# Local and downsampled attention with two MLP layers: loads and GpSimd adds join the written order of the opening

## The chip, the cores and the metric

The kernel runs on one core of one Trainium2 chip. The metric is the device time of one execution in microseconds. Five engines matter here: PE (TensorE) multiplies, ACT (ScalarE) and DVE (VectorE) do the elementwise work, POOL (GpSimd) adds, and SP (SyncE) issues nearly all the DMAs.

## The reference

Four batches, eight heads, 576 positions, head size 64. The output of attention is a local part plus a coarse part; it runs through two MLP layers over all 2304 tokens.

```python
q_d, k_d, v_d = means of q, k, v over groups of 4 positions        # 144 of them
out_d     = softmax(scale * q_d @ k_d.T) @ v_d
out_up    = repeat(out_d, 4)                                       # back to 576
out_local = softmax(where(|i - j| < 4, scale * q @ k.T, -1e6)) @ v
x = (out_up + out_local) as 2304 x 512
h = x @ w_in            # 512 -> 2048
x = (h * sigmoid(1.702 * h)) @ w_out
h = x @ w2_in
y = where(h > 0, h, exp(min(h, 0)) - 1) @ w2_out
```

The weights arrive as 64-bit floats, and the kernel turns them into pairs of single-precision parts on the chip.

## The kernel before, in words

**Units.** Attention goes by unit: one batch and two heads (a head pair, four per batch). Of batch 0 a unit is split: `e0` to `e3` are windows 0 to 3 of its four head pairs (64 rows by 70 keys each) and its downsampled half, `l0` to `l3` are windows 4 to 8. `r0` to `r3` are the four head pairs of batch 1. The other batches come later, between the blocks of the first MLP layer, and are laid out by a planner that the change does not touch.

**A unit's steps** are tokens with the unit's name behind them. `Tq`/`Tk` turn a piece of q or k on PE (`turn_piece`, L506), `Cq`/`Ck` copy it from PSUM on ACT (L518; for `Cq.e0` on DVE, L516), `Sq`/`Sk` sum four positions on DVE (L522). `QK` makes the local scores (L550 mask, L559 product), `NM` their negative maximum on DVE (L586), `EW` the exponentials on ACT (L623). `QD`, `ND`, `NS`, `EC` are the same for the downsampled scores (L602, L609, L614, L630). `W`, `MS`, `MP` weigh both by the reciprocal of their sums on DVE (L661, L662, L665). `PD`/`PC` and `PT`/`PTC` turn the weights (L686/L694 and L704/L709/L711), `PVD` and `DN` make the downsampled result (L720, L728), `PV` and `X` the local one and the sum (L741, L756). `PVD` needs `vd`, the sums of four positions of v: for each of the unit's two heads (a half) one load of a tile `vr` (L469) and three additions on GpSimd (L474, L476). `PV` needs `vw`, the windows of v, four DMAs per unit (L486).

**The weights** come in chunks of 512 KB (`wst1i`, `wst1o`; L188, L193). `A1` (ACT, L212), `D1` and `DS` (DVE, L215), `D2` (DVE, L230), `A3` (ACT, L237) and `D3` (DVE, L241) convert one.

**The first MLP layer** runs in blocks of 256 or 512 tokens. In the opening blocks 0 and 1 go together: `H.s.p` is half p of step s of the first product (L993), `TH`, `ST`, `GH`, `GL` its gate (L1002, L1006, L1012, L1019), `Y.s.h` half h of the second product (L1060). Steps 0 to 7 cover 256 tokens and two chunks of weights, steps 8 to 15 both blocks and one chunk. `XH`/`XL` split the attention result into a high and a low part (L384, L388). `*N` is N filler products of 448 columns on PE (`keep_busy`, L1104), whose result nobody reads.

**What sets the order.** `OPENING` (L66 to L107) lists the tokens of blocks 0 and 1; a loop issues them one after the other inside `manual_schedule`, which keeps the written order on PE, ACT and DVE. For SP and GpSimd the order is the framework's. Loads have no tokens: those of the early units, six weight chunks and the first `vw` of a late unit stand in a fixed block ahead of the table (L1115 to L1133), and each further one hangs on a step: a weight chunk on `D2`, the next unit's q and k on the fourth turning, its `vw` on `PV`, a later unit's `vr` and its additions on `DN` (L730). The pool `att` has one tile `vr` for the units `r*`, and one tile `vw` that `e0`, the late units and the `r*` take in turn.

Of the kernel before, what the change touches and what calls it, by code (L numbers as in the profile page):

```python
# [50 lines left out]
LOADS = 6  # L51
# [20 lines left out]
    W.e0 ND1.e3 EW.e3 *1 PD0.e1 MP.e0 NS.e3 W.e2 PD0.e0 EC.e3 MS.e0 PD1.e0 PTC.e1 MP.e2 *1 PT.e0 PC0.e1 MS.e2
    PC0.e0 PD0.e2 PC1.e0 W.e3 PD1.e1 PD1.e2 PC0.e2 DS.1 PT.e2 PC1.e2 PTC.e0 PVD.e0 A1.1 MP.e3 PVD.e2 PC1.e1 DN.e0
    MS.e3 A1.2 PD0.e3 PTC.e2 PD1.e3 A3.0 PT.e3 D1.2 DN.e2 PVD.e1 PC1.e3 D2.1 PV.e2 DN.e1 PTC.e3 PC0.e3 PV.e0 X.e2
    DS.2 PV.e1 D1.3 PV.e3 X.e1 PVD.e3 D2.2 XH.01 XH.02 QK.l1 D3.0 A3.1 X.e0 A3.2 QK.l0 XL.02 A1.3 XL.01 NM.l1
    XH.00 D1.4 DN.e3 NM.l0 DS.3 EW.l0 D3.1 XL.00 D1.5 EW.l1 *11 H.0.0 W.l0 D2.3 H.0.1 MS.l0 A1.4 X.e3 PTc.l0
# [10 lines left out]
    A1.15 ST.5 QD0.r1 A3.14 D1.15 H.7.0 D3.13 DS.15 Ma.r1 D3.14 QD1.r1 A1.16 ST.4 H.7.1 A1.17 D2.15 GH.4 D1.16
    A3.15 H.6.0 ND1.r1 DS.16 ND0.r1 NS.r1 D3.15 EC.r1 H.6.1 D1.17 D2.16 MS.r0 A1.18 QKb.r1 A3.16 D1.18 PD1.r0
    Y.2.0 DS.17 Mb.r1 D3.16 PC1.r0 GL.4 PTa.r0 A1.19 D1.19 Tq0.r2 TH.6 Y.2.1 D2.17 DS.18 PTCa.r0 ST.6 A3.17 PVD.r0
    DS.19 D2.18 H.8.0 D3.17 Cq0.r2 D2.19 A3.18 Tq1.r2 H.8.1 A3.19 D3.18 DN.r0 A1.20 D3.19 PTb.r0 GH.5 D1.20 Y.3.0  # L90
    Cq1.r2 Na.r1 PTCb.r0 GL.5 EWa.r1 Nb.r1 Tk0.r2 Sq.r2 Y.3.1 EWb.r1 D1.21 TH.7 D1.22 Tk1.r2 Y.4.0 EWc.r1 ST.7
    D1.23 A1.21 H.9.0 W.r1 Ck1.r2 D1.24 Ck0.r2 MP.r1 GH.6 Y.4.1 Sk.r2 A1.22 GL.6 DS.20 PD0.r1 MS.r1 QD0.r2 PC0.r1
    Y.5.0 GH.7 ND0.r2 D2.20 DS.21 QD1.r2 A3.20 H.9.1 ND1.r2 NS.r2 D2.21 EC.r2 D1.25 Y.5.1 D3.20 TH.8 GL.7 A1.23
    PTc.r0 PVa.r0 PTCc.r0 DS.22 ST.8 QKa.r2 Xa.r0 D1.26 GH.8 Y.6.0 A3.21 Ma.r2 D2.22 TH.9 PD1.r1 DS.23 D3.21
    QKb.r2 GL.8 H.10.0 PC1.r1 Mb.r2 A1.24 ST.9 A3.22 Tk0.r3 Nb.r2 Tq0.r3 Na.r2 Ck0.r3 Y.6.1 D1.27 Cq0.r3 D2.23
    EWa.r2 PVD.r1 D1.28 A3.23 Tq1.r3 D3.22 Y.7.0 DN.r1 Cq1.r3 D1.29 DS.24 D3.23 PVb.r0 D1.30 Tk1.r3 Xb.r0 H.11.0
# [22 lines left out]
def kernel(  # L119
# [275 lines left out]
    class Unit:  # L395


        def __init__(self, b, hp, w0, w1, down=None):
# [36 lines left out]
        def load_qk(self):  # L435
            self.raw = []
            b, hp = self.b, self.hp
            if self in turned:
# [11 lines left out]
            for nm, src in (("q", q), ("k", k)):  # L450
                r = self.t([96, 6, 2, D], f"raw{nm}")

                queue = nc.scalar if self in early[:2] and nm == "k" else nc.sync
                for j in range(2):
                    queue.dma_start(
                        out=r[:, :, j, :], in_=src[b, 2 * hp + j].rearrange("(p t) d -> p t d", t=6)
                    )
                self.raw.append(r)
        def add_vd(self):

            b, hp = self.b, self.hp
            self.vd = self.t([HALF, 2, 2, D], "vd", bufs=2)
            for j in range(2):
                tag = ("gh", "gl", "gh", "g")[self.hp] if j == 0 else ("gh", "gl", "gl", "g")[self.hp]
                if self in early:
                    r = gpool.tile([HALF, 2, 4, D], F32, tag=tag, name=f"vr{j}_{self.n}", bufs=2 if tag == "g" else None)
                else:
                    r = att.tile([HALF, 2, 4, D], F32, tag="vr", name=f"vr{j}_{self.n}")
                nc.sync.dma_start(  # L469
                    out=r.rearrange("g c r d -> g c (r d)"),  # L470
                    in_=v[b, 2 * hp + j].rearrange("(c g r) d -> g c (r d)", g=HALF, r=4),
                )
                vd = self.vd[:, :, j, :]
                nc.gpsimd.tensor_tensor(out=vd, in0=r[:, :, 0, :], in1=r[:, :, 1, :], op=ALU.add)  # L474
                for i in (2, 3):
                    nc.gpsimd.tensor_tensor(out=vd, in0=vd, in1=r[:, :, i, :], op=ALU.add)  # L476
# [919 lines left out]
```

## Time and profile before

| what | value |
|---|---|
| median of 3 runs | 975.35 us (974.5 to 976.1) |
| the profiled execution, its own time | 974.49 us |
| its span | 972.3 us, mean granted TensorE clock 0.981 |
| PE busy in the span | 948.0 us, 97% |
| DVE, ACT, POOL busy | 503.8, 466.6, 60.8 us |
| first product of the MLP (`H.0.0`) | at 49.95 us |
| last product of a unit of the opening (`PVb.r3`) | at 190.01 us |

The profiled execution is 0.86 us under the median. Granted clock 1.00 means 2.4 GHz and 0.50 means 1.2 GHz. In the views of the trace an idle time in brackets stands before the work that followed it, with what that work was waiting for.

### The profile page before, as it was taken

What the parts mean: (1) busy time and instruction counts of PE and PEld (TensorE: products, weight loads), DVE (VectorE), ACT (ScalarE), POOL (GpSimd) and SP (SyncE); (2) the same over time, 40 slices, a digit from 0 to 9 for tenths busy, and PEclk for the clock granted to TensorE, in tenths of its full rate; (3) what the DMA queues carried; (4) which work ended last, traced back from release to release, by engine and by line L of the source; (5) the groups of instructions that cost most, each with busy time, mean ns of one, the idle gap of its engine ahead of it and who ended that gap; (6) DMA issues with size and microseconds to landing.
All of it is one profiled execution on the core that took longest, in us unless ns stands there. A gap on an engine that the chain in (4) does not pass through costs nothing. (4 is left out here: it accounts for less than half of the span.)

```text
span 972.3 us, 14685 instructions
## 1 busy us (share of the span) xinstructions
PE 948.0 (97%) x5773; PEld 775.6 (80%) x5773; DVE 503.8 (52%) x900; ACT 466.6 (48%) x1115; POOL 60.8 (6%) x117
## 2 busy tenths in 40 slices
PE   8978999999999999999999999999999999999998
PEld 5758987777777778888888978877888888888897
DVE  5888997676654543223225898884223222322232
ACT  5667999464343532232225566664334333433343
POOL 4330110201111010000000000000000000000000
PEclk9588999999999999999999999999999999999999
DMA  9587712153222204010007921002001100100010
GB/s 192 162 232 205 232 31 55 46 116 64 52 55 46 70 20 144 1 43 1 1 1 240 366 88 43 1 12 77 1 1 38 39 1 1 55 0 1 1 44 22
DMA packets 113332, 67.97 MB, mean 70 GB/s; under 512 B 80752, under 2 KB 102768, under 8 KB 113264
## 3 DMA queue, kind: packets, MB, share of 16 engines
q1 hardware_dynamic: 110896, 66.46, 24.3%
q10 hardware_dynamic: 2368, 0.59, 0.4%
q8 instruction: 45, 0.74, 0.3%
q14 instruction: 23, 0.19, 0.1%
HBM read 57.59 MB, written 9.44 MB: 69 GB/s over the span
## 5 line engine op out<-in xcount | busy, mean ns | idle before, releaser
L1245 PE MATMUL o<-whl2o,g2h 128*128 128x512 f32 x576 | 181.0, 394 | 2.4 <-ACT ye L1072 2.1
L1196 PE MATMUL h<-x2h,whl2i 128*128 128x512 f32 (+1 forms) x640 | 159.3, 371 | 0.0
L1060 PE MATMUL y<-g1h,whl1o 128*128 128x512 f32 (+1 forms) x512 | 156.2, 371 | 0.0
L993 PE MATMUL h<-xh,whl1i 128*128 128x512 f32 (+1 forms) x640 | 147.1, 354 | 2.4 <-DVE g L1006 2.4
L1206 DVE SCALAR_TENSOR_TENSOR g<-e,h 128x512 f32<-128x512 f32 (+1 forms) x80 | 50.7, 634 | 177.9 <-ACT e L1204 177.6
L1196 PEld LDWEIGHTS h<-x2h,whl2i 128*128 128x128 f32 x640 | 114.7, 189 | 22.7
L1245 PEld LDWEIGHTS o<-whl2o,g2h 128*128 128x128 f32 x576 | 107.2, 189 | 27.1 <-ACT ye L1072 2.5
L993 PEld LDWEIGHTS h<-xh,whl1i 128*128 128x128 f32 x640 | 105.8, 190 | 19.4 <-DVE g L1006 3.3
L1203 ACT ACTIVATE e<-h 128x512 f32<-128x512 f32 (+1 forms) x80 | 44.3, 554 | 158.3 <-PE h L1196 158.3
L1245 PE MATMUL o<-whl2o,g2l 128*128 128x512 f32 x288 | 113.1, 393 | 0.0
L1060 PEld LDWEIGHTS y<-g1h,whl1o 128*128 128x128 f32 x512 | 92.4, 189 | 16.3 <-issue 1.2
L1006 DVE SCALAR_TENSOR_TENSOR g<-g,h 128x512 f32<-128x512 f32 x64 | 43.8, 684 | 118.9 <-ACT g L1002 118.9
L1002 ACT ACTIVATE g<-h 128x512 f32<-128x512 f32 x64 | 38.1, 596 | 122.7 <-PE h L993 115.9
L1060 PE MATMUL y<-g1l,whl1o 128*128 128x512 f32 (+1 forms) x256 | 93.7, 366 | 0.0
L1196 PE MATMUL h<-x2l,whl2i 128*128 128x512 f32 (+1 forms) x320 | 79.6, 370 | 0.0
L993 PE MATMUL h<-xl,whl1i 128*128 128x512 f32 (+1 forms) x320 | 77.6, 354 | 0.0
L1213 DVE TENSOR_TENSOR g2l<-g,g2h 128x512 fp32r<-128x512 f32 (+1 forms) x80 | 51.7, 646 | 36.8 <-ACT g2h L1211 21.6
L1211 ACT ACTIVATE g2h<-g 128x512 fp32r<-128x512 f32 (+1 forms) x80 | 47.1, 589 | 42.8 <-DVE g L1206 42.7
L1196 PEld LDWEIGHTS h<-x2l,whl2i 128*128 128x128 f32 x320 | 56.7, 188 | 11.0
L1245 PEld LDWEIGHTS o<-whl2o,g2l 128*128 128x128 f32 x288 | 54.4, 189 | 12.0
L993 PEld LDWEIGHTS h<-xl,whl1i 128*128 128x128 f32 x320 | 53.2, 191 | 7.3 <-issue 0.4
L1019 DVE TENSOR_TENSOR g1l<-g,g1h 128x512 fp32r<-128x512 f32 x64 | 44.2, 691 | 27.7 <-ACT g1h L1012 27.4
(128 smaller groups left out, 1326.2 us busy)
## 6 DMA issues: line engine op xcount, KB each, us to landing
wst1i<-in_moe_w_in_dram SPq DMA_DIRECT2D x16, 512.0 KB
wst1o<-in_moe_w_out_dram SPq DMA_DIRECT2D x16, 512.0 KB
wst2i<-in_moe_w_in_dram SPq DMA_DIRECT2D x16, 512.0 KB
wst2o<-in_moe_w_out_dram SPq DMA_DIRECT2D x16, 512.0 KB
vr<-in_v_dram SPq DMA_DIRECT2D x32, 144.0 KB
out_dram<-ot SPq DMA_DIRECT2D x18, 256.0 KB
y<-ydram SPq DMA_DIRECT2D x16, 256.0 KB
ydram<-ye SPq DMA_DIRECT2D x14, 256.0 KB
```

Of the source, the lines that this page charges most:

```text
L993: nc.tensor.matmul(out=hps[blk, fs][:, i, :], lhsT=w_in(1, f, c, wp), rhs=columns(xp, c), start=(n == 0), stop=(n >= len(todo) - nf), skip ...
L1002: return nc.scalar.activation(out=g, in_=hps[blk, fs], func=AF.Tanh, scale=0.851)
L1006: return nc.vector.scalar_tensor_tensor(out=g, in0=g, scalar=1.0, in1=ph, op0=ALU.add, op1=ALU.mult)
L1019: return nc.vector.tensor_tensor(out=gl, in0=g, in1=gh.bitcast(F32), op=ALU.subtract)
L1060: nc.tensor.matmul(out=sums(m), lhsT=w_out(1, f, wp)[:, m, :], rhs=gp[:, i, :], start=(opens and n == 0 and m % per == 0), stop=(last and ...
L1196: nc.tensor.matmul(out=ph[:, :n], lhsT=w_in(2, f, c, wp), rhs=xp[:, c, :n], start=(i == 0), stop=(i == 3 * NK - 1),)
L1203: nc.scalar.activation(out=e[:, :n], in_=ph[:, :n], func=AF.Relu, scale=-1.0)
L1206: urgent["dve"] = nc.vector.scalar_tensor_tensor(out=g[:, :n], in0=e[:, :n], scalar=-1.0, in1=ph[:, :n], op0=ALU.add, op1=ALU.max)
L1211: nc.scalar.activation(out=gh[:, :n], in_=g[:, :n], func=AF.Copy)
L1213: return lambda: nc.vector.tensor_tensor(out=gl[:, :n], in0=g[:, :n], in1=gh[:, :n].bitcast(F32), op=ALU.subtract)
L1245: nc.tensor.matmul(out=ops[bi][i], lhsT=gp[:, i * P:(i + 1) * P], rhs=wo[wp], start=(f == 0 and m == 0), stop=(f == NF - 1 and m == 2),)
```

## The change

The table of the opening is written anew, with six new kinds of tokens: `LW` loads the next weight chunk, `LQ` and `LK` q or k of a unit, `VW` its four windows of v, `VD0` and `VD1` one half of `vr`, and `GA0` and `GA1` the three additions of a half. The fixed block of loads and the loads that hung on `D2`, `PV`, `DN` and the fourth turning go (those of the units after the opening stay), and SP and GpSimd take their order from the table too. The late units' maxima `nm` take the early unit's tile in place of one of their own. The same instructions run on PE, DVE and ACT in both, but for the fillers: 34 in place of 38 (besides 15 at the start). After the opening PE, ACT and DVE have the same sequence as before.

```diff
 OPENING = """
-    Tq0.e0 Tk0.e0 Cq0.e0 Tk1.e0 Ck0.e0 Tq1.e0 Ck1.e0 Cq1.e0 Sk.e0 *3 Tq0.e1 Tk0.e1 Sq.e0 Cq0.e1 Tq1.e1 Tk1.e1
...
+    LW.0 LQ.e3 LK.e3 Tq0.e0 Tq1.e0 Cq0.e0 LW.1 Tk0.e0 Cq1.e0 LK.e2 Tk1.e0 Ck0.e0 Sq.e0 Ck1.e0 *2 Tq0.e1 Tq1.e1
...
 """.split()
-                self.nm = self.t([P, NWIN], "nm", bufs=4)
+                self.nm = self.dn_from.nm if self in late else self.t([P, NWIN], "nm", bufs=4)
...
             at = whole.index(self) + 2
-            if NHP <= at < len(whole):
+            if self in turned and at < len(whole):
                 whole[at].add_vd()
...
+            if step == "LQ" and self in turned:
+                self.load_qk()
+            elif step in ("LQ", "LK"):
+                self.load_raw("QK".index(step[1]))
+            elif step == "VW":
+                self.load_v()
+            elif step in ("VD0", "VD1"):
+                self.load_half(int(step[2]))
+            elif step in ("GA0", "GA1"):
+                self.add_half(int(step[2]))
...
-                    self.nturned += 1
-                    if self.nturned == 4 and self in rest:
-                        nxt.load_qk()
...
-                if part != "a" and self not in early:
-                    nxt.load_v()
...
-    with tc.manual_schedule(engines={ET.PE, ET.Activation, ET.DVE}):
+    with tc.manual_schedule(engines={ET.PE, ET.Activation, ET.DVE, ET.Pool, ET.SP}):
...
-        early[0].add_vd()
-        early[0].load_v()
-        early[2].load_qk()
-        early[3].load_qk()
-        wt1.load(1)
-        early[1].add_vd()
-        early[1].load_v()
-        wt1.load(1)
-        for u in early[2:]:
-            u.add_vd()
-            u.load_v()
-        wt1.load(2)
-        late[0].load_v()
-        wt1.load(LOADS)
-        rest[0].load_qk()
...
-                if step == "D2":
-                    wt1.load()
+            elif step == "LW":
+                wt1.load()
```

Three places in the order. **DVE, its first steps.** Before, from its sixth instruction on (`kd_1`, `qs_1`, `qkd_0_1` are e1's; `qkd_0_0`, `qk_0_0` e0's):

```order
L522 TENSOR_REDUCE kd_1_0_307<-kd_1_0_307 128x144
L522 TENSOR_REDUCE kd_1_0_307<-qs_1_0_302 128x144
L609 TENSOR_REDUCE nmd_1_0_355<-qkd_0_1_0_357 72x2
L609 TENSOR_REDUCE nmd_1_0_355<-qkd_0_1_0_367 72x2
L614 TENSOR_SCALAR nmd_1_0_355<-nmd_1_0_355 72x4
L586 TENSOR_REDUCE nm_1_0_376<-qk_0_1_0_377 128x4
```

And after the change, from the sixth on:

```order
L601 TENSOR_REDUCE nm_0_0_222<-qk_0_0_0_223 128x4
L537 TENSOR_REDUCE kd_1_0_237<-qs_1_0_207 128x144
L624 TENSOR_REDUCE nmd_0_0_243<-qkd_0_0_0_245 72x2
L220 TENSOR_SCALAR wst1i_168<-wst1i_168 128x512
L624 TENSOR_REDUCE nmd_0_0_243<-qkd_0_0_0_260 72x2
L629 TENSOR_SCALAR nmd_0_0_243<-nmd_0_0_243 72x4
```

The maxima of e0's own scores and the first step on a weight chunk now stand where e1's sums stood; that step on the weights (`D1.0`) was DVE's twentieth instruction and is its ninth.

**SP, from the late unit l1 on.** Before (`vw_1_4` is l1's windows, `vr_1_0` and `vr_1_1` the halves of r0 and r1 of batch 1; a wait names the queue slot or engine waited for):

```order
L469 DMA vr_1_0_0_651<-in_v_dram 72x2x256 [waits DMAHW6_49,DMAHW3_49,Pool_49]
L188 DMA wst1i_814<-in_moe_w_in_dram 128x4x128 [waits DMAHW7_49,DVE_49]
L486 DMA vw_1_4_860<-in_v_dram 70x4x64 [waits DMAHW0_49,PE_49]
L469 DMA vr_1_1_0_767<-in_v_dram 72x2x256 [waits DMAHW6_49,DMAHW1_49,Pool_49]
L486 DMA vw_1_4_860<-in_v_dram 70x64 [waits DMAHW2_49]
L486 DMA vw_1_4_860<-in_v_dram 70x4x64
L486 DMA vw_1_4_860<-in_v_dram 70x64 [waits DMAHW4_49]
```

After:

```order
L462 DMA rawq_1_0_799<-in_q_dram 96x6x64 [waits DMAHW3_49]
L501 DMA vw_1_4_848<-in_v_dram 70x4x64 [waits DMAHW5_49,DMAHW6_49,DMAHW4_49,PE_49]
L501 DMA vw_1_4_848<-in_v_dram 70x64
L501 DMA vw_1_4_848<-in_v_dram 70x4x64
L501 DMA vw_1_4_848<-in_v_dram 70x64 [waits DMAHW7_49]
L193 DMA wst1i_876<-in_moe_w_in_dram 128x4x128 [waits DMAHW0_49]
L193 DMA wst1i_885<-in_moe_w_in_dram 128x4x128 [waits DMAHW1_49]
L198 DMA wst1o_892<-in_moe_w_out_dram 128x512 [waits DMAHW2_49]
```

A load of `vr` that waits for GpSimd stood between l1's first and second load of windows; now the four stand together, and the next `vr` comes behind three weight chunks and l2's windows.

**PE, ahead of the first product of the MLP.** Before (`qk_0_0_4` is l0's scores; the two rows of `busy` stand eleven times):

```order
L550 MATMUL qk_0_0_4_745<-mask,identb 128x350
L559 MATMUL qk_0_0_4_745<-kT_0_0_280,qT_0_0_275 64x70 x10
L1104 LDWEIGHTS ones
L1104 MATMUL busy<-ones 128x448
...
L993 MATMUL h_0_0_804<-xh_719,whl1i_635 128x256
```

After:

```order
L521 MATMUL pt_1_0_0_782<-ident,rawq_0_0_479 128x96 x3
L756 MATMUL pv_0_2_0_789<-vp_2_0_514 64x64 x8
L565 LDWEIGHTS identb
L565 MATMUL qk_0_2_4_804<-mask,identb 128x350
L574 MATMUL qk_0_2_4_804<-kd_2_0_365,qs_2_0_406 64x70 x10
L756 MATMUL pv_0_0_4_824<-PT_0_4_697,vw_0_4_688 64x64 x10
L1013 MATMUL h_0_0_840<-xh_737,whl1i_477 128x256
```

The eleven fillers ahead of `H.0.0` are gone (29 of the new table's 34 stand farther ahead, in groups of one to six, and five behind; before, a group of 17 stood among the first turnings), and l0's own `PV`, l2's scores and all four turnings of r0 now come before `H.0.0`.

## Rows read from the trace of the kernel before

**Rows 1.** The page: busy time of two engines, and the granted clock in 40 slices.
```profile
PE 948.0 (97%) x5773; PEld 775.6 (80%) x5773; DVE 503.8 (52%) x900; ACT 466.6 (48%) x1115; POOL 60.8 (6%) x117
PEclk9588999999999999999999999999999999999999
```

**Rows 2.** Stretches: start:end, length, busy us of each engine (instructions), clock, DMA share, GB/s.
```profile
7.29:20.00 12.71, 11.95 (x106) 8.09 (x106) 8.09 (x17) 9.00 (x27) 2.77 (x7) 1.00 1.14 218
20.00:30.00 10.00, 7.61 (x90) 5.41 (x85) 9.93 (x26) 9.43 (x50) 8.45 (x13) 0.92 0.68 160
30.00:50.00 20.00, 19.78 (x184) 14.92 (x182) 15.26 (x30) 10.79 (x41) 3.64 (x6) 0.53 0.57 185
50.00:60.00 10.00, 9.36 (x103) 8.47 (x102) 9.92 (x23) 7.41 (x21) 2.70 (x3) 1.00 1.04 280
60.00:75.00 15.00, 8.58 (x78) 7.35 (x77) 10.67 (x23) 8.29 (x30) 5.39 (x10) 0.77 0.68 197
75.00:93.00 18.00, 15.26 (x150) 13.45 (x149) 13.94 (x31) 12.64 (x37) 0.00 (x0) 0.81 0.70 176
93.00:130.00 37.00, 37.00 (x317) 34.34 (x315) 35.80 (x66) 36.83 (x83) 4.05 (x6) 1.00 0.64 201
130.00:191.00 61.00, 61.00 (x520) 48.91 (x519) 45.15 (x89) 48.95 (x118) 9.20 (x17) 1.00 0.18 39
191.00:960.00 769.00, 763.34 (x4181) 625.03 (x4180) 351.41 (x597) 318.32 (x708) 19.87 (x38) 1.00 0.18 51
```

**Rows 3.** Timeline of DVE: start, busy us, engine, line, operation [idle before, released by].
```profile
12.08 0.75 DVE L522 TENSOR_REDUCE kd<-kd 128x144 f32<-128x576 f32 x1 [1.91 <-ACT kd L518]
14.89 0.45 DVE L609 TENSOR_REDUCE nmd<-qkd 72x2 f32<-72x288 f32 x1 [1.40 <-PE qkd L602]
20.55 0.73 DVE L215 TENSOR_SCALAR wst1i<-wst1i 128x512 uint16<-128x512 uint16 x1
```

**Rows 4.** Timeline of SP's DMA queue: the issues, and the gap from 29.69 to 41.12.
```profile
13.98 0.63 SPq L188 DMA_DIRECT2D wst1i<-in_moe_w_in_dram  x1
27.64 2.05 SPq L188 DMA_DIRECT2D wst1i<-in_moe_w_in_dram  x4
41.12 1.82 SPq L486 DMA_DIRECT2D vw<-in_v_dram  x4
...
65.15 0.32 SPq L469 DMA_DIRECT2D vr<-in_v_dram  x1
65.52 1.28 SPq L486 DMA_DIRECT2D vw<-in_v_dram  x3
```

**Rows 5.** Timelines of PE and of DVE: the waits around the late unit l1's windows.
```profile
68.31 1.33 PE L741 MATMUL pv<-PT,vw 70*64 70x64 f32 x18 [3.13 <-DMA vw<-in_v_dram]
69.68 0.56 DVE L756 TENSOR_TENSOR x<-pv,dn 128x256 f32<-128x256 f32 x2 [3.02 <-PE pv L741]
```

**Rows 6.** Timeline of PE: one group of turnings, fillers, first MLP product, `Y.3.0`, last unit product.
```profile
15.82 0.47 PE L506 MATMUL pt<-ident,rawk 96*128 96x96 f32 x3
47.21 3.06 PE L1104 MATMUL busy<-ones 128*128 128x448 bf16 x11
49.95 0.44 PE L993 MATMUL h<-xh,whl1i 128*128 128x256 f32 x1
119.70 0.36 PE L1060 MATMUL y_both<-g1h,whl1o 128*128 128x256 f32 x1
190.01 0.69 PE L741 MATMUL pv<-PT,vw 70*64 70x64 f32 x16
```

**Rows 7.** Groups of DVE by shape, 93 to 190 us: mean ns of one `D1`/`DS`.
```profile
L215 DVE TENSOR_SCALAR wst1o<-wst1o 128x512 uint16<-128x512 uint16 x12 | 9.5, 791 | 0.0
```

**Rows 8.** The granted clock in the stretch where it was half (columns as in Rows 2).
```profile
28.30:48.90 20.60, 19.72 (x184) 15.35 (x185) 15.84 (x32) 11.06 (x41) 5.26 (x8) 0.50 0.56 173
```

**Rows 9.** GpSimd's additions by line, first in 9 to 36 us, then in 93 to 191.
```profile
L474 POOL TENSOR_TENSOR vd<-vr 72x128 f32<-72x128 f32 x8 | 5.2, 647 | 12.7 <-DMA vr<-in_v_dram 12.7
...
L474 POOL TENSOR_TENSOR vd<-vr 72x128 f32<-72x128 f32 x8 | 4.7, 582 | 102.9 <-PE pvd L720 92.8 <-DMA vr<-in_v_dram 10.2
```

More of the change, by code (lines that the diff above doesn't have):

```diff
@@ L72 @@
[L72 to L76, printed above, removed]
@@ L87 @@
[L87 to L91, printed above, removed]
@@ L92 @@
[L92 to L96, printed above, removed]
@@ new lines @@
+    GA1.e0 VD0.e2 *3 PD0.e1 PC0.e0 Sk.e2 PT.e0 A3.0 LQ.r0 QK.l0 Cq1.e2 NS.e3 MS.e1 EC.e3 PTC.e0 QK.e2 VW.e2 GA0.e1
+    Sq.e2 PD1.e1 NM.l0 PC0.e1 *1 QD0.e2 PC1.e1 NM.e2 EW.l0 D1.2 LW.5 QD1.e2 GA0.e0 ND0.e2 W.e3 ND1.e2 EW.e2 *3
+    Tk0.r0 W.l0 PD1.e0 MS.e3 QK.l1 GA0.e3 NS.e2 MP.e3 Ck0.r0 EC.e2 DS.2 PT.e1 NM.l1 GA0.r0 D3.0 EW.l1 *4 PD0.e3
+    PTC.e1 PT.e3 W.e2 D1.3 GA1.e1 PC1.e0 *3 PD1.e3 PC0.e3 MS.e2 Tk1.r0 PC1.e3 PVD.e0 PTC.e3 PT.e2 MS.l0 DN.e0
+    Ck1.r0 PV.e0 MP.e2 A1.2 PVD.e1 VW.l0 X.e0 A1.3 PTC.e2 PTc.l0 GA0.e2 PD0.e2 PVD.e3 A3.1 PTCc.l0 W.l1 DN.e1
@@ new lines @@
+    Cq0.r2 GL.4 A1.17 D2.16 Tk0.r2 TH.6 PD1.r0 H.7.1 D1.18 Ck0.r2 D3.15 PC1.r0 A3.16 D1.19 A1.18 Tk1.r2 ST.6
+    Tq1.r2 DS.17 LK.r3 Y.2.0 D3.16 MS.r0 A1.19 LQ.r3 D2.17 DS.18 H.8.0 Na.r1 D1.20 LW.31 A3.17 Y.2.1 D2.18 DS.19
+    D1.21 Ck1.r2 D3.17 H.8.1 A3.18 D2.19 Cq1.r2 D3.18 PTb.r0 A3.19 D1.22 PVD.r0 PTCb.r0 D3.19 GH.5 GA0.r2 PTa.r0
+    Nb.r1 EWa.r1 Y.3.0 GL.5 Sk.r2 TH.7 PTCa.r0 DN.r0 VD1.r2 EWb.r1 Y.3.1 ST.7 D1.23 A1.20 Sq.r2 EWc.r1 H.9.0 D1.24
+    GH.6 W.r1 Y.4.0 A1.21 MP.r1 GA1.r2 DS.20 GL.6 D1.25 PD0.r1 QD0.r2 PC0.r1 D2.20 TH.8 QD1.r2 VD0.r3 ND0.r2 DS.21
@@ new lines @@
+    Ck1.r3 LQ.r4 GH.10 A1.27 GL.10 H.11.0 EWc.r2 D3.25 Sk.r3 A1.28 PVD.r1 D1.31 QKa.r3 DN.r1 GA0.r3 DS.26 QD0.r3
+    Ma.r3 DS.27 Na.r3 QD1.r3 ND0.r3 Y.8.1 VD1.r3 ND1.r3 DS.28 W.r2 NS.r3 D2.26 EC.r3 H.11.1 MS.r2 MP.r2 A3.26
+    Y.9.0 EWa.r3 GA1.r3 PD0.r2 PVa.r1 PC0.r2 TH.11 QKb.r3 Xa.r1 PVb.r1 Mb.r3 D3.26 PD1.r2 VW.r2 H.12.0 D2.27 A1.29
+    Nb.r3 A3.27 ST.11 EWb.r3 Y.9.1 D3.27 Xb.r1 PC1.r2 D2.28 EWc.r3 H.12.1 GH.11 W.r3 PTa.r2 A3.28 GL.11 PTb.r2
+    TH.12 PTCa.r2 H.13.0 PTCb.r2 MP.r3 A1.30 ST.12 DS.29 PTc.r2 PVD.r2 D3.28 H.13.1 GH.12 PTCc.r2 VD0.r4 D2.29
@@ L107 @@
+    DS.30 MS.r3 Y.10.0 A3.29 D2.30 DN.r2 TH.13 D3.29 H.14.0 A1.31 GL.12 A3.30 GA0.r4 ST.13 Y.10.1 VD1.r4 PD0.r3
+    PVa.r2 PC0.r3 DS.31 PVb.r2 Xa.r2 PD1.r3 Xb.r2 GH.13 Y.11.0 D3.30 PC1.r3 D2.31 GL.13 H.14.1 GA1.r4 A3.31 Y.11.1
+    TH.14 ST.14 PTc.r3 PVD.r3 PTCc.r3 PTa.r3 DN.r3 VD0.r5 GH.14 PTb.r3 VW.r3 PTCa.r3 Y.12.0 PTCb.r3 GL.14 D3.31
+    H.15.0 GA0.r5 Y.12.1 H.15.1 VD1.r5 Y.13.0 TH.15 ST.15 PVa.r3 GH.15 PVb.r3 Xa.r3 GA1.r5 Y.13.1 Xb.r3 VW.r4
+    GL.15
 """.split()
@@ L447, in load_qk @@
                         )
-                    self.raw.append(r)
+                    self.raw[nm == "k"] = r
                 return
[L450 to L458, printed above, removed]
+            for which in range(2):
+                self.load_raw(which)
@@ L459, in add_vd, with load_raw @@
+        def load_raw(self, which):
+            nm, src = (("q", q), ("k", k))[which]
+            r = self.t([96, 6, 2, D], f"raw{nm}")
+            queue = nc.scalar if self in early[:2] and which == 1 else nc.sync
+            for j in range(2):
+                queue.dma_start(
+                    out=r[:, :, j, :], in_=src[self.b, 2 * self.hp + j].rearrange("(p t) d -> p t d", t=6)
+                )
+            self.raw[which] = r
         def add_vd(self):
-            b, hp = self.b, self.hp
@@ L462, in add_vd @@
-            self.vd = self.t([HALF, 2, 2, D], "vd", bufs=2)
             for j in range(2):
[L464 to L476, printed above, removed]
+                self.load_half(j)
@@ new lines, in add_vd, with load_half @@
+                self.add_half(j)
+        def load_half(self, j):
+            tag = ("gh", "gl", "gh", "g")[self.hp] if j == 0 else ("gh", "gl", "gl", "g")[self.hp]
+            if self in early:
+                r = gpool.tile([HALF, 2, 4, D], F32, tag=tag, name=f"vr{j}_{self.n}", bufs=2 if tag == "g" else None)
+            else:
+                r = att.tile([HALF, 2, 4, D], F32, tag="vr", name=f"vr{j}_{self.n}")
+            nc.sync.dma_start(
+                out=r.rearrange("g c r d -> g c (r d)"),
+                in_=v[self.b, 2 * self.hp + j].rearrange("(c g r) d -> g c (r d)", g=HALF, r=4),
+            )
+            self.halves[j] = r
@@ L478, in load_v, with add_half @@
+        def add_half(self, j):
+            if self.vd is None:
+                self.vd = self.t([HALF, 2, 2, D], "vd", bufs=2)
+            r, vd = self.halves.pop(j), self.vd[:, :, j, :]
+            nc.gpsimd.tensor_tensor(out=vd, in0=r[:, :, 0, :], in1=r[:, :, 1, :], op=ALU.add)
+            for i in (2, 3):
+                nc.gpsimd.tensor_tensor(out=vd, in0=vd, in1=r[:, :, i, :], op=ALU.add)
         def load_v(self):
@@ L770, in one @@
             kind = step[:-1] if part else step
-            if step[0] == "T" or step[:2] in ("Cq", "Ck"):
+            if step == "LQ" and self in turned:
[8 more added lines that the diff above has]
+                self.add_half(int(step[2]))
+            elif step[0] == "T" or step[:2] in ("Cq", "Ck"):
                 which, i = "qk".index(step[1]), int(step[2])
```

55 lines of the change are left out of this document (27 added, 28 removed).

## The prediction

> **What bounds the kernel now.** I read the page first, then the stretches of time, then the timelines of PE, DVE and SP. The page says that PE is the bound as a whole, 948.0 of 972.3 us, and that its granted clock is low in the second to fourth of 40 slices and nowhere else [rows 1]. The stretches say where PE isn't full: from 93 us on it is busy in every microsecond of the opening, and in 763.34 of 769 us after it [rows 2]. The change touches the opening alone, and what follows has the same sequence on the compute engines. So whatever the opening's end gains is carried to the end one to one, and the question is only when the opening ends: the last product of a unit there starts at 190.01 us [rows 6].
>
> Before 93 us nothing is full for long. PE is idle for 0.8, 2.4, 0.2, 0.6, 6.4 and 2.7 us in the six stretches from 7.29 to 93, 13.1 us in all, has half the clock for 20.6 us [rows 8], and spends time on 38 fillers. It has slack to give. DVE is the engine to count: it is busy 9.93 of 10 us and 9.92 of 10 us in two stretches, 35.80 of 37 us from 93 to 130, and idle for 4.62, 0.07, 4.74, 0.08, 4.33 and 4.06 us in the six stretches ahead of 93 [rows 2], together 17.9 us. The weights cause this: every chunk costs DVE four instructions, and PE's last long run of work can only begin when most are converted. From 130 us on DVE is idle for a quarter of the time and PE for none. So I take the end of the opening as the sum of three things: DVE's work up to `Y.3.0`, DVE's idle time ahead of it, and PE's work from there (119.70 to about 190.7 us, 71 us [rows 6]). A token moved only matters if it changes one of the three.
>
> **The change part by part.**
>
> *The lead-in, 7.29 to 20 us.* DVE waits 1.91 us for a copy and 1.40 us for a product, both of unit e1, while the first step on a weight chunk comes only at 20.55 us [rows 3]: that chunk was issued at 13.98 us [rows 4], behind the loads of four q and k. The new order puts the maxima of e0 there, which need e0 alone, and has the chunk issued first on SP, some 7 us earlier; `D1.0` is DVE's ninth instruction. The loads move 218 GB/s in this stretch already [rows 2], so bringing the chunk forward (512 KB, 2.4 us at that rate) holds e2's and e3's q and k back by about as much; their turnings stand farther back as well. Of 4.62 us I leave 2.2: two short chains through PE, ACT and DVE at the start, of about the length of the 1.40 us wait, less some overlap. Bounds 0 and 4.6. **Minus 2.4.**
>
> *20 to 50 us.* SP issues nothing between 29.69 and 41.12 us [rows 4], because the next entry of its queue, l0's windows, waits for e0's `PV`. PE crawls at half the clock from 28.3 to 48.9 us [rows 8] with few gaps, so whatever DVE needs from PE comes late: 4.74 us idle from 30 to 50 [rows 2]. In the new order the wait for `PV.e0` is behind the q of r0 and six weight chunks, and DVE has conversions to do in between. But ACT was busy 9.43 of 10 us from 20 to 30 [rows 2] and now gets l0's and l1's exponentials earlier too. I leave 2.0 of 4.7. Bounds 1.0 and 4.7 (nothing gained). **Minus 2.7.** `H.0.0`, at 49.95 us before [rows 6], should then start near 46.
>
> *60 to 93 us.* Three of l1's four loads of windows go out at 65.52 us, behind a load of `vr` at 65.15 that waits for GpSimd [rows 4]. So l1's `PV` waits 3.13 us for them, and DVE 3.02 us for that `PV` [rows 5]. The new queue has l1's four loads in a row, and the next `vr` farther back. What stays is the shared tile: l2's windows can only be loaded after l1's `PV`, about 1.8 us of issue [rows 4] and a landing, but the new order has all that spread from `H.0` to `H.2`. What is late next there is `W` and `MS` of the late units behind their exponentials on ACT. Of 8.39 us idle I leave 4.0. Bounds 1.5 and 8.4. **Minus 4.4.**
>
> *DVE's work ahead of `Y.3.0`.* The new table has two more `D1` (D1.21, D1.22) ahead of it, 0.79 us each [rows 7]; one maximum comes ahead and one copy goes behind, which I set equal. Two turnings of r2 leave PE's tail, at most 0.47 us each [rows 6], taken as 0.5 together. **Plus 1.1.** Four fillers fewer, and the shared `nm`, I cost at nothing: PE's slack covers the first, and the late unit's maxima come after the early unit's last use of the tile in the order of both tables. If that cover is gone it costs the wait of one 0.4 us reduction.
>
> *GpSimd's additions.* One takes 647 ns on average at 9 to 36 us, and 582 ns at 93 to 191 us, though DVE is busier there [rows 2, 9]. So company of DVE costs an addition a tenth at most, and the 27 additions up to e2's last half end some 17 us after they begin, in time for `PVD.e2`. The Trainium skill, SBUF — State Buffer, section "Who interferes with whom", says that an instruction of VectorE with two SBUF inputs holds the port pair that it shares with GpSimd, and that the loser is fully blocked. Were every addition blocked once for one DVE instruction, they would take twice as long; the rows above show a tenth, so the sum goes by the rows and the rule is priced as a rival.
>
> The sum is 2.4 + 2.7 + 4.4 - 1.1 = 8.4 us less. The profiled execution took 974.49 us, so 966.1; it is 0.86 us under the median of the runs, and on the median's footing the forecast is **967.0 us**. The bounds of the three idle terms together (2.5 to 17.7 us left of 17.9) give 961.2 to 976.4.
>
> **The rivals.**
>
> *Better still (chance 0.14).* PE keeps the full clock, because the fillers are spread, and DVE's chains close up: 4.5 us idle in place of 8.2, so 963.3 or somewhat less. For it: after 93 us DVE runs at 97% for 37 us [rows 2]. Against it: in the first 20 us nothing but the chain of one or two units can run.
>
> *The clock falls all the same and comes back with the MLP (0.16).* Before, it fell at 28.3 us, when PE had been busy for 7.61 of 10 us, and came back at 48.9 us, within the eleven fillers that start at 47.21 [rows 2, 6, 8]. Between the last group of three fillers and `H.0.0` the new order has no filler. If the clock is half from some 34 us to `H.0`, the middle term is lost and part of the third: 4 us gained, 971.4.
>
> *Slower: the clock stays low past `H.0.0` (0.11).* This is the same mechanism from another point on. The eleven fillers ahead of `H.0.0` are gone, and `H.0` and `H.1` are mixed with late-unit products and waits. PE's work from 30 to about 75 us, where `H.2` ends before, is at the full clock: half of 19.78 less 3.06 of fillers, 8.4; 9.36; and from 60 to 75, 8.58 less about 2 for a low clock there: 24.4 us [rows 2, 6]. Some 3 us of unit products moved ahead of `H.2` and about 3 us already done by 34 us cancel. At half the clock that takes 48.8 us from 34 on and ends at 83, 8 us later than before. DVE is starved for that long and makes up perhaps 2.6 us of its old idle time afterwards; with the 1.1 us of order the opening ends 6.5 us later, 981.9. It decides if the clock isn't back by the middle of `H.1`. Against it: PE was dense at the full clock right after 50 us, 9.36 of 10, and `H.0` is a dense run in the new order too.
>
> *The loads were hidden anyway (0.11).* The table moves tokens, but the opening keeps DVE waiting elsewhere, and only l1's wait of 3.02 us goes, less 1.1: 973.4, no change that shows.
>
> *The adds block (0.03).* By full blocking, 27 additions take 19 us more, e2's `PVD` comes some 16 us late and `H.0.0` with it; less the 8.4 that is 7.6 us slower, 982.9. The tenth in [rows 9] speaks against it.
>
> **How the numbers follow.** The forecast itself has the remaining 0.45. Two parts in a thousand, 1.95 us, is what a measurement of this kernel can tell from no change. Faster by more than that: the forecast, less 0.02 of its own upper end, the better case, and 0.15 of the early fall of the clock, together 0.72. Within it: the hidden loads, with 0.02 from each side's edges, 0.13. Slower: the low clock, the adds and 0.01 for a wait that I don't see, 0.15. The range leaves out the slow cases beyond 976.5 (0.14) and the far end of the better one (0.04): 960.5 to 976.5.
>
> **What the profile will show.** If I am right, `D1.0` starts by 14 us, SP issues l1's four windows within 2 us of one another, SP has no gap of 11 us before 45 us, `H.0.0` starts between 45 and 47 us, DVE is idle for 8 to 9 us in all from 7.29 to 93 us (17.9 before), and the last product of a unit of the opening starts near 181.6 us. The forecast is wrong if the granted clock is half past `H.0.0`, if DVE's idle time ahead of 93 us stays above 14 us, or if the opening's end gains and the end of the kernel doesn't.

## The result: 15.6 us faster, nearly twice the forecast

The changed kernel takes 960.15 us (median of 4 runs, 956.44 to 964.33), the kernel before 975.73 us beside it; the ratio is 0.9843 (95% interval 0.9801 to 0.9885). The forecast was 967.0, the range 960.5 to 976.5: the median lies 0.35 us under the range. The profiled execution took 960.35 us. One execution among the experiments (the profiled one of `e13`) ran at a granted clock of about 0.75 throughout and took 1153.71 us; it stands in none of the figures below.

The page, the lines of [rows 1]:

```profile
PE 938.1 (98%) x5769; PEld 768.2 (80%) x5769; DVE 502.2 (52%) x900; ACT 465.5 (49%) x1115; POOL 69.4 (7%) x117
PEclk9899999999999999999999999999999999999999
```

The stretches, with the columns of [rows 2]:

```profile
7.29:20.00 12.71, 11.35 (x115) 7.87 (x115) 11.32 (x24) 10.82 (x37) 2.15 (x2) 1.00 1.20 235
20.00:30.00 10.00, 9.79 (x128) 6.83 (x122) 9.87 (x25) 10.00 (x51) 8.70 (x16) 1.00 0.97 214
30.00:50.00 20.00, 18.44 (x206) 14.57 (x202) 17.41 (x38) 14.45 (x52) 8.67 (x13) 0.76 0.80 187
50.00:60.00 10.00, 9.82 (x138) 7.91 (x136) 8.72 (x22) 6.82 (x21) 0.72 (x1) 0.96 0.74 218
60.00:75.00 15.00, 13.75 (x126) 12.35 (x121) 15.00 (x33) 13.24 (x42) 6.97 (x5) 1.00 0.92 271
75.00:93.00 18.00, 16.06 (x141) 14.52 (x140) 17.93 (x35) 15.94 (x30) 2.57 (x2) 1.00 0.86 265
93.00:130.00 37.00, 32.42 (x307) 29.11 (x307) 31.93 (x61) 33.79 (x75) 5.49 (x6) 1.00 0.55 133
...
40.00:50.50 10.50, 10.48 (x102) 8.92 (x103) 7.98 (x18) 5.85 (x19) 2.32 (x5) 0.52 0.85 215
```

DVE is idle for 1.39, 0.13, 2.59, 1.28, 0.00 and 0.07 us ahead of 93 us, 5.5 in all (17.9 before). PE's clock is half once, for 10.5 us. Before, it was half three times, in the stretch of [rows 8] and in these two:

```profile
66.00:72.60 6.60, 4.29 (x45) 3.73 (x46) 2.35 (x7) 1.77 (x6) 2.09 (x5) 0.50 0.74 220
79.50:86.40 6.90, 6.34 (x43) 5.76 (x44) 3.77 (x8) 2.96 (x10) 0.00 (x0) 0.51 0.87 281
```

From 93 to 130 us there is a loss that the kernel before hasn't: PE is idle for 4.6 us and DVE for 5.1. PE's timeline shows it, with `H.0.0`, `Y.3.0` and the last product of a unit:

```profile
47.11 0.58 PE L1013 MATMUL h<-xh,whl1i 128*128 128x256 f32 x1
...
95.62 0.44 PE L521 MATMUL pt<-ident,rawq 96*128 96x96 f32 x3 [1.90 <-DMA rawq<-in_q_dram]
99.90 0.44 PE L521 MATMUL pt<-ident,rawk 96*128 96x96 f32 x3 [2.39 <-DMA rawk<-in_k_dram]
...
110.04 0.36 PE L1080 MATMUL y_both<-g1h,whl1o 128*128 128x256 f32 x1
...
177.59 1.27 PE L756 MATMUL pv<-PT,vw 70*64 70x64 f32 x36
```

r2's q and k are late. The timelines of GpSimd and of SP's queue say why:

```profile
69.02 2.04 POOL L489 TENSOR_TENSOR vd<-vr 72x128 f32<-72x128 f32 x1 [7.79 <-DMA vr<-in_v_dram]
71.14 6.51 POOL L491 TENSOR_TENSOR vd<-vd,vr 72x128 f32<-72x128 f32 x2
```

```profile
65.84 0.93 SPq L193 DMA_DIRECT2D wst1i<-in_moe_w_in_dram  x2
77.67 0.33 SPq L479 DMA_DIRECT2D vr<-in_v_dram  x1
78.05 0.84 SPq L198 DMA_DIRECT2D wst1o<-in_moe_w_out_dram  x2
...
82.56 4.71 SPq L462 DMA_DIRECT2D rawq<-in_q_dram  x2
```

Three additions of r1's second half take 8.6 us while DVE has no gap. SP stands before r2's first half of v (`VD0.r2`), which needs the same tile, until 77.67 us (its issue before ends at 66.77 us, and the load that the additions need lands at 69.0); eight weight chunks and r2's q then crowd behind it.

The balance of the profiled executions, 14.1 us: DVE's idle time ahead of `Y.3.0` falls from 18.4 us (112.4 us less 94.0 busy) to 8.7, 9.7 us less; its work there is 94.0 us in both; PE's time from `Y.3.0` to the product after the last `PV` falls from 70.9 to 68.8, 2.2 less; the rest, behind the opening, takes 2.0 us less, 1.6 of it in PE's waits for the step `ST` of the gate on DVE (2.4 to 0.8 us), and what lies around the span 0.3.

The runs of the changed kernel lie 8 us apart, and follow the mean granted clock. With the four of a second measurement there are eight: 955.75 us at 1.000, 956.44 at 0.998, 956.41 at 0.996, 959.95 and 960.35 at 0.993, 962.54 at 0.991, 961.87 at 0.989, 964.33 at 0.988. That is some 0.7 us for each 0.001.

> The changed kernel itself once more, beside the others on one chip, since its runs lie 8 us apart (956.4 to 964.3 at clocks of 0.998 to 0.988). Theory: the time follows the clock, some 0.8 us for each 0.001, and a run at a clock of 0.993 takes 959 to 961. Rival: the times spread as much at one clock.

Measured: 959.14 us (955.75 to 962.54), ratio 0.9833 (0.9785 to 0.988). The first theory holds, if not closely: the time at 0.991 lies above that at 0.989. The profiled execution of this measurement is the one at the full clock, 955.75 us:

```profile
20.00:30.00 10.00, 10.00 (x130) 7.15 (x128) 9.85 (x25) 10.00 (x51) 9.14 (x18) 1.00 0.98 216
30.00:50.00 20.00, 17.95 (x242) 14.16 (x238) 19.67 (x44) 16.05 (x58) 8.60 (x12) 1.00 0.85 198
50.00:60.00 10.00, 8.00 (x109) 6.35 (x108) 8.49 (x21) 6.70 (x19) 1.36 (x3) 1.00 0.99 261
```

Here DVE is idle for 2.0 us from 20 to 60 us, against 4.0 where the clock fell.

### The profile page after: what moved, and what is told of

Read it like the earlier page. It is cut to its first block, busy times and chain, and to the rows that moved or that the text cites. A ratio compares the mean times of both kernels' runs of the same rounds, so it can differ in the third digit from the quotient of the medians.

```text
span 958.5 us, 14665 instructions
## 1 busy us (share of the span) xinstructions
PE 938.1 (98%) x5769; PEld 768.2 (80%) x5769; DVE 502.2 (52%) x900; ACT 465.5 (49%) x1115; POOL 69.4 (7%) x117
```

## The experiments

### Steps and loads, one without the other

`e4_old_steps_new_loads`: the old table's steps, with the new load tokens merged into it in their new order. `e5_new_steps_old_loads`: the kernel before with the new table, its load tokens left out.

```diff
 e4:  OPENING = the old steps and fillers, with LW LQ LK VW VD GA in the new order
 e5:  OPENING = the new steps and fillers, loads as in the kernel before
```

> The steps of PE, ACT and DVE and the fillers in the order of the kernel before, with the loads and GpSimd's additions in the order of the changed kernel (three weight chunks a little earlier where the old order needs them). Theory (the loads carry the gain): DVE's idle time ahead of 93 us falls from 17.9 to 12 us or less, and the time is 965 to 970. Rival (the order of the steps carries it, and loads alone do nothing): within 2 us of 975, or slower, since e1's and e2's steps now wait for loads that come later than their turn.

> The steps and fillers of the changed kernel, with the loads issued as in the kernel before (the fixed block at the start, the rest hung on steps, SP and GpSimd ordered by the framework). Theory (the loads carry the gain): the new steps then wait for their data, first for q and k of e3, which come behind e2's, and for the first chunk of weights at 14 us and later; DVE's idle time ahead of 93 us is above 12 us and the time is 970 or more. Rival (the order of the steps carries it): 965 or less.

Measured: new loads alone 981.12 us (977.07 to 983.6), ratio 1.0058 (1.004 to 1.0077), slower. New steps alone 972.43 us (969.74 to 975.58), 0.9964 (0.9948 to 0.998). Together they give 15 us. e4's rival holds, in its slower form: PE waits 6.33 us for a q at 20.51 us. So does e5's theory: PE waits 9.06 us for a k at 48.32 us, and DVE is idle for 23.9 us from 7.29 to 93 us. Neither half carries the gain by itself, and the parts aren't a sum. The stretches of e4, then of e5:

```profile
7.29:20.00 12.71, 5.94 (x42) 3.46 (x40) 4.17 (x6) 3.59 (x6) 0.90 (x2) 0.85 1.19 223
20.00:30.00 10.00, 9.49 (x48) 6.34 (x49) 3.34 (x8) 5.04 (x20) 7.04 (x16) 0.50 1.00 216
```

```profile
7.29:20.00 12.71, 6.99 (x73) 4.63 (x71) 3.79 (x7) 4.72 (x14) 2.56 (x6) 0.96 1.01 211
60.00:75.00 15.00, 14.06 (x198) 11.20 (x197) 13.98 (x35) 11.99 (x40) 2.71 (x3) 1.00 0.57 148
75.00:93.00 18.00, 15.43 (x160) 13.85 (x159) 17.12 (x37) 14.02 (x44) 2.02 (x3) 1.00 0.66 188
```

In both DVE does only some 4 us of work in the first 12.7, since steps and loads stand in different orders and each step waits. `H.0.0` starts at 61.63 and 64.22 us. Behind it the new steps are fast with the old loads too: from `H.0.0` to `H.8.0` e5 takes 53.9 us, the changed kernel 56.8, the kernel before 66.2, e4 63.3. In part that may be the later start, which gives the loads 17 us more; the two aren't told apart.

### SP and GpSimd left to the framework

```diff
-    with tc.manual_schedule(engines={ET.PE, ET.Activation, ET.DVE, ET.Pool, ET.SP}):
+    with tc.manual_schedule(engines={ET.PE, ET.Activation, ET.DVE}):
```

> The changed kernel with its table, but SP and GpSimd not held to it: the framework orders them. Its SP order differs only by a few loads (k of r0 and of r2 earlier or later by a few places). Theory: the gain is in where the loads stand in the table and in the new steps, not in holding SP and GpSimd to it; 958 to 963, like the changed kernel. Rival: holding them is what gives the gain; then at least half of the 15 us is lost (967 or more) and a wait for a load appears on PE or DVE ahead of 93 us.

Measured: 957.76 us (955.78 to 960.93), 0.9819 (0.9788 to 0.9851). The theory holds, a little below its 958 to 963: holding the two engines to the table shows no gain beside the places of the load tokens.

### The late loads back on their steps

`e9_old_triggers`: the new steps and early loads, the later loads where the old triggers put them.

> The steps of the change, the loads of the early units, the first six weight chunks, and r0's q and k at their new places; every later load hung on a step as in the kernel before (weights on D2, q and k on the fourth turning, windows on PV, v with its additions on DN), and SP and GpSimd ordered by the framework. Theory: the steps carry the gain behind H.0.0 and the new early loads the gain ahead of it, so that where the later loads stand is worth little: H.0.0 at 46 to 48 us, 956 to 963. Rival: the later loads' places matter as well, a load that waits for GpSimd blocks l1's windows or the weights again, DVE is idle for over 4 us from 60 to 93 us, and the time is 966 or more.

Measured: 966.81 us (964.46 to 968.57), 0.991 (0.9879 to 0.9941). The rival holds: DVE is idle for 6.6 us from 60 to 93 us. `H.0.0` is at 46.90 us, but SP's queue and PE show the old trouble, larger:

```profile
54.78 0.33 SPq L480 DMA_DIRECT2D vr<-in_v_dram  x1
...
58.80 0.31 SPq L480 DMA_DIRECT2D vr<-in_v_dram  x1
59.16 1.77 SPq L502 DMA_DIRECT2D vw<-in_v_dram  x4
```

```profile
63.41 1.62 PE L757 MATMUL pv<-PT,vw 70*64 70x64 f32 x20 [9.96 <-DMA vw<-in_v_dram]
```

l1's windows stand behind loads of v that wait for GpSimd. In the changed kernel they go out at 47.25 us. All the later loads moved here, so that the price of this one wait isn't told apart from that of the others.

### The blocked queue in the old order

`e3_vr_r1` moves r1's loads of v out of the way of l1's windows, `e13_vr_r0_r1` those of r0 and r1.

```diff
-            if NHP <= at < len(whole):
+            if NHP <= at < len(whole) and whole[at] not in rest[:2]:
...
                     nxt.load_v()
+                if self in late[2:]:
+                    rest[late.index(self) - 2].add_vd()
```

> The kernel before with one load moved: r1's two halves of v are loaded and added behind X.l1, not at DN.e3, so that no load that waits for GpSimd stands among l1's four loads of windows. This is the third term of the prediction by itself. Theory: l1's PV no longer waits 3.13 us for its windows, DVE no longer 3.02 us; the time falls by 2 to 4 us (971 to 973). Rival: with the gap of PE the low clock from 66 to 72.6 us goes too, and the time falls by 5 us or more. Other rival: the next wait ends at the same place, and the time stays within 1 us of 975.

> The kernel before with r0's halves of v loaded and added at PV.l2 and r1's at PV.l3, so that no load that waits for GpSimd stands ahead of or among l1's four loads of windows (with r1's alone moved, r0's second half still held them until 64.5 us). Theory (the third term of the prediction, the blocked queue, is worth 4 us in the old order): SP issues l1's windows in a row by 58 us, PE's and DVE's waits of 3 us there go, 969 to 971. Rival (in the old order other waits lie right behind: 60 to 93 us keeps over 5 of 8.4 us of DVE's idle time): 972 to 975.

Measured: e3 970.14 us (965.56 to 974.27), 0.9964 (0.9939 to 0.9989). That lies between its theory and its first rival. In its profiled execution, of 973.93 us, PE still waits 5.46 us for l1's windows: r0's second half does what r1's did:

```profile
63.65 0.32 SPq L469 DMA_DIRECT2D vr<-in_v_dram  x1
...
64.54 1.82 SPq L486 DMA_DIRECT2D vw<-in_v_dram  x4
```

e13 takes 968.44 us (median of three runs, 965.86 to 968.92), 0.9926 (0.9903 to 0.995), 5 to 9 us less by the interval: its theory holds, and a little more. What became of its waits isn't shown by a trace of its own; that of e14, below, has the same moved loads.

### The fillers and the clock

`e6_before_fill`: the kernel before with 18 more fillers. `e14_vr_fill`: e13 with the same. `e7_no_fill`: the changed kernel with none.

```diff
 e6, e14:  ... *6 PD0.e0 ... *3 PD0.e2 ... *3 PT.e3 ... *3 PV.e2 ... *3 QK.l1 ...
 e7:       every *N of the table left out
```

> The kernel before with 18 more fillers on PE, six in its wait of 1.4 us ahead of PD0.e0 and three each ahead of PD0.e2, PT.e3, PV.e2 and QK.l1; nothing else. Theory (the clock carries much of the gain): the granted clock stays full through most of 28 to 49 us, H.0.0 starts at 46 us or earlier, and the time is 970 or less. Rival (the loads and the order carry it; the low clock filled time that PE had to wait in anyway): the clock is higher, but PE waits instead, and the time is within 2 us of 975.

> The same, with the 18 more fillers ahead of H.0.0 as well. Theory (the clock ahead of H.0.0 and the blocked queue behind it are two separate losses): their gains add up, about 3 from the fillers and what the moved loads give alone, 964 to 968. Rival (both are the same slack): no better than the better of the two by over 1 us.

> The changed kernel without its 34 fillers in the opening (the 15 at the start stay). Theory (the clock carries much of the gain): the clock falls by 20 us and stays low to 50 or 60 us, as with the steps of the change and the old loads; the time is 966 to 972. Rival (the order is dense enough to hold the clock or not to need it): 958 to 962.

Measured: e6 971.28 us (969.2 to 974.58), 0.9978 (0.996 to 0.9997); e14 963.1 us (960.97 to 965.75), 0.9879 (0.9851 to 0.9908); e7 964.74 us (962.64 to 967.05), 0.9901 (0.987 to 0.9932). e14's theory holds, and a little more; e6 and e7 lie between their theory and their rival. The stretches of e6, and its SP queue:

```profile
30.00:50.00 20.00, 17.73 (x225) 12.98 (x225) 18.31 (x41) 14.07 (x53) 4.53 (x8) 1.00 0.68 223
...
60.00:75.00 15.00, 10.11 (x93) 8.99 (x93) 9.77 (x20) 7.45 (x26) 4.81 (x9) 0.66 0.84 214
```

```profile
28.55 2.06 SPq L189 DMA_DIRECT2D wst1i<-in_moe_w_in_dram  x4
39.79 2.04 SPq L487 DMA_DIRECT2D vw<-in_v_dram  x4
```

The clock is full to 50 us, and DVE's idle time from 30 to 50 us falls from 4.7 to 1.7 with the old order and the old loads, although SP's queue still has its gap, from 30.61 to 39.79 us: that part of the loss belonged to the clock, not to the gap. (From 7.29 to 50 us in all it falls less, from 9.4 to 7.7, since 1.1 us more is lost from 20 to 30.) `H.0.0` comes at 45.64 us. But the wait for l1's windows is still there, 2.49 us on PE, and the low clock with it (0.66). With both edits l1's four windows go out in a row from 54.55 us, and DVE's idle time from 60 to 93 us falls from 8.4 to 2.5, though PE still waits 1.81 us for them. The stretches of e14:

```profile
30.00:50.00 20.00, 19.24 (x221) 13.47 (x219) 18.00 (x39) 12.89 (x54) 5.27 (x8) 0.90 0.59 189
...
60.00:75.00 15.00, 11.07 (x137) 9.23 (x136) 12.51 (x31) 11.03 (x35) 0.00 (x0) 0.89 0.84 217
75.00:93.00 18.00, 17.51 (x160) 16.35 (x160) 17.95 (x38) 17.33 (x48) 10.49 (x7) 1.00 0.59 170
```

The gains add up at the least: 0.0022 from the fillers, 0.0074 from the queue, 0.0121 from both; the intervals are too wide to say that both give more than the sum. So two small edits in the old order give about three quarters of the change's 0.0157. In the changed kernel, e7 shows that its fillers are worth 5 to 6 us: without them the clock falls in the first stretches.

```profile
20.00:30.00 10.00, 10.00 (x78) 7.42 (x76) 7.75 (x16) 7.07 (x31) 8.83 (x18) 0.50 0.94 206
```

### The loss that the change brought

`e1_vr_r2` moves one token; `e12_add_dve` has r1's second half added on DVE.

```diff
 e1
-... Y.0.1 VD0.r2 ST.1 ... XL.13 LK.r2 QKa.r1 ...
+... Y.0.1 ST.1 ... XL.13 LK.r2 VD0.r2 QKa.r1 ...
 e12, in add_half
+            eng = nc.vector if self is rest[1] and j == 1 else nc.gpsimd
...
-                nc.gpsimd.tensor_tensor(out=vd, in0=vd, in1=r[:, :, i, :], op=ALU.add)
+                eng.tensor_tensor(out=vd, in0=vd, in1=r[:, :, i, :], op=ALU.add)
```

> The changed kernel with one token moved: r2's first half of v (VD0.r2) is loaded after r2's k (LK.r2), not ahead of ten weight chunks. In the changed kernel SP waits there for GpSimd from about 67 to 77.7 us while three additions take 8.6 us, the DMA engines stand still from about 72 to 77 us, and r2's q and k land at 95.6 and 99.9 us, which PE waits for (1.90 and 2.39 us). Theory: the blocked additions are what delays q and k; with the load moved, SP goes on issuing at 67 us, both waits of PE go, DVE's idle time from 93 to 130 us falls from 5.1 to under 2 us, and the time falls by 3 to 5 us against the changed kernel at the same clock (956). Rival: the weight chunks wait for their tiles or for DVE anyway, q and k come as late as before, and the time stays within 1 us of 960.

> The changed kernel with the three additions of r1's second half of v on DVE, not GpSimd. In the changed kernel they take 8.6 us on GpSimd, from 69.0 to 77.65 us, while DVE has no gap. Theory (GpSimd is held up by DVE): on DVE the three take under 1 us, SP issues r2's first half of v by 71 us and the ten weight chunks behind it, r2's q and k land at least 4 us earlier, and the time falls by 1 to 4 us although DVE has more to do. Rival (the load of v that lands at 69 us is late, and the additions are slow of themselves): the three take 2 us or more on DVE as well, and the time stays or rises by what DVE does more.

Measured: e1 955.36 us (952.62 to 957.97), 0.9791 (0.9758 to 0.9824); e12 957.43 us (955.9 to 960.15), 0.9818 (0.9782 to 0.9854). e1's SP queue and its stretch from 93 us:

```profile
75.63 3.88 SPq L463 DMA_DIRECT2D rawq<-in_q_dram  x2
...
84.82 0.59 SPq L480 DMA_DIRECT2D vr<-in_v_dram  x1
```

```profile
93.00:130.00 37.00, 35.91 (x318) 32.35 (x319) 34.99 (x66) 36.68 (x82) 5.75 (x6) 1.00 0.37 90
```

PE is idle for 1.1 us there (4.6 in the changed kernel) and DVE for 2.0 (5.1); both waits of PE are gone, as the theory has it. GpSimd's two additions take 6.51 us in e1 as well, but no load waits for them. In e12 DVE makes the same three in 0.90 us, and SP goes on at 69.08 us:

```profile
68.13 0.29 DVE L490 TENSOR_TENSOR vd<-vr 72x128 f32<-72x128 f32 x1 [1.68 <-DMA vr<-in_v_dram]
68.45 0.61 DVE L492 TENSOR_TENSOR vd<-vd,vr 72x128 f32<-72x128 f32 x2
```

```profile
69.08 0.33 SPq L479 DMA_DIRECT2D vr<-in_v_dram  x1
...
76.41 4.77 SPq L462 DMA_DIRECT2D rawq<-in_q_dram  x2
```

So GpSimd's additions, more than the load, held the queue. In e12 the load shows up elsewhere: DVE waits 1.68 us for it, and PE 2.47 us for DVE's gate behind that.

A full DVE isn't enough to make the additions slow. In e2, where `VD0.r2` stands at the same place, the same three took 2.0 us beside the same steps of DVE, which has no gap there either:

```profile
68.53 0.46 POOL L489 TENSOR_TENSOR vd<-vr 72x128 f32<-72x128 f32 x1 [7.01 <-DMA vr<-in_v_dram]
69.06 1.52 POOL L491 TENSOR_TENSOR vd<-vd,vr 72x128 f32<-72x128 f32 x2
```

```profile
60.00:75.00 15.00, 13.71 (x132) 12.26 (x128) 15.00 (x33) 12.95 (x40) 3.25 (x6) 1.00 1.05 323
```

There SP went on at 70.61 us, and PE was idle for 1.1 us from 93 to 130 us, as in e1: a second sign that the held queue is what made r2's q and k late. Of the seven traces of the changed kernel and its near variants that add on GpSimd, five have the slow additions (7.8 to 8.6 us for the three) and two, e2 and e10, the fast ones (2.0 and 2.4). What decides between them isn't shown.

How much of the gains of e1 and e12 is the edit and how much a better clock in these runs isn't settled: at 0.993 e1 took 957.97 us (the changed kernel 959.95 and 960.35), at full clock 953.89 and 952.62 (955.75), but at 0.996 both are at 956 to 957.

### Two tries for more

```diff
 e8:   e1, with *3 ahead of PTb.l0, *3 ahead of Tq0.r0, *2 ahead of QK.l2
 e10:  e1, with LQ.r0 ahead of VW.e3
```

> The changed kernel with r2's first half of v loaded behind r2's k, and 8 more fillers between 35 and 46 us, where the clock fell in the profile of the changed kernel (three ahead of PTb.l0, three ahead of Tq0.r0, two ahead of QK.l2). Theory: the clock stays full in all runs, and the time is 951 to 954 in each, against 952.6 to 958.0 without the fillers. Rival: the fillers cost 1.5 us of PE and the clock falls in some runs all the same; median 955 or more.

> The changed kernel with r2's first half of v behind r2's k, and r0's q loaded ahead of e3's windows: it lands at 40 us in the changed kernel, where PE waits 0.78 us for it and the clock falls. Theory: that wait goes, the clock stays full in more runs, 951 to 954 in most. Rival: e3's and e0's windows come later for it and their PV waits; 955 or more, as without the move.

Measured: e8 956.55 us (954.03 to 958.83), 0.9816 (0.9783 to 0.9848); e10 956.44 us (953.92 to 959.34), 0.9806 (0.9768 to 0.9844). The times of both rivals hold: nothing over e1. e10's rival named another wait than the one that came: in its profiled execution PE no longer waits for r0's q, nor for windows up to `H.0.0`, but 1.42 us for GpSimd's sums ahead of `PVD.e2`. The clock was below 0.995 in one run of four of e8 and in three of e10. e1 is the best version found; its interval overlaps those of the changed kernel, e8 and e10.

## Why the prediction fell short

The sign and the mechanism were right: the opening's end moved and was carried to the end, by DVE's idle time. The sum was 8.4 us for 14.1 in the profiled execution. Most of the sizes were off, and some cancelled: 4.7 us of idle time, in the second term and from 93 us on, came out worse than forecast, and 10.3 us in the other rows better. That the total still lies so near the range is in part luck. Step by step:

| step | forecast | measured |
|---|---|---|
| lead-in, DVE idle left | 2.2 | 1.4 |
| 20 to 60 us, idle left | 2.1 | 4.0 |
| 60 to 93 us, idle left | 4.0 | 0.07 |
| 93 us to `Y.3.0`, idle | not named (0.5 before) | 3.3 |
| DVE's work ahead of `Y.3.0` | plus 1.6 | 0.0 |
| PE from `Y.3.0` | minus 0.5 | minus 2.2 |
| behind the opening | 0 | minus 2.3 |

- **The third term failed most.** I left 4.0 of 8.4 us, with `W` and `MS` behind ACT as what is late next, and wrote minus 4.4. For DVE nothing was late next: 0.07 is left, minus 8.3. The blocked queue alone is worth 5 to 9 us in the old order (e13). I wrote little more than l1's own wait of 3 us; the clock, too, is half from 66.0 us, within that wait of PE, to 72.6, and DVE's waits behind it [rows 2, 5] went as well. That the clock is what made the rest of the term is argued: no run kept the wait and held the clock up behind it.
- **The second term had the wrong cure.** I named PE's half clock as what keeps DVE waiting, but took the gain from loads that get past SP's gap [rows 4]. e6 takes 3 us of the 4.7 away with fillers alone, the gap still there; and in the changed kernel, whose queue has no such gap, 4.0 us are left where the clock falls. At the full clock 2.0 are left, as forecast (2.1). My rival of the falling clock came to pass as a stretch of 10.5 us, and at about its price: the run at full clock is some 4 us faster than those at 0.993.
- **The fourth term didn't come.** Two more `D1` do stand ahead of `Y.3.0`, yet DVE's busy time up to there is 94.0 us in both. The steps `MP` take 0.74 to 0.81 us each now, and four of five took 0.92 to 1.02 before, which is part of it; why wasn't tried.
- **PE's work from `Y.3.0`** fell by 2.2 us, not 0.5. The six products of r2's two turnings are 0.9 us of it by their busy time; the rest is the same products, a little shorter each (the 45 of `y_both` with 512 columns 401 ns for 414), and why stays open.
- **The end behind the opening** gained 2.3 us where I wrote one to one. The 1.6 of fewer waits for `ST` is seen; why it comes with the change stays open.
- **The rival of blocked additions** was priced at the wrong place. I rejected it with [rows 9], which compare two averages that both had DVE's company; against the 0.45 us of a fast addition they are 29 and 44% more. In the changed kernel the three additions at 69 us take 8.6 us, those at 59 us 1.9. No addition kept `PVD.e2` waiting there; those at 69 us held up SP's queue, some 30 us later. The rule that I priced (the Trainium skill, SBUF — State Buffer, "Who interferes with whom") speaks of VectorE's instructions with two SBUF inputs. The trace agrees in that additions are held up beside DVE, 8.6 us for three where DVE is busy for 15.00 of 15 us; but e2, with DVE as busy and 2.0 us for the same three, shows that this alone doesn't settle it.
- **The slow clock past `H.0.0`** lasted 3.4 us, from 47.11 to 50.5 us; from there on the clock was full, and the rival did not come.
- **The other signs.** `D1.0` (12.39 us), l1's windows (all four within 1.71 us) and the queue without a gap came as said. `H.0.0`, at 47.11 us, came just behind its 45 to 47; DVE's idle time ahead of 93 us, 5.5, and the last product, at 177.59 us, came out lower than I wrote.

The range was too narrow below for two reasons: the third term went past its bound (0.07 left, 1.5 at the least in the forecast), and the fourth term and what follows `Y.3.0` were held as certain. With runs 8 us apart, which side of the lower end a single run falls on is chance: five of the eight lie under it, three inside.
